# Windowed attention and a gelu MLP on one core: one group of blocks of the first products as seven block products in five more tiles

## The chip, the core and the metric

The kernel runs on 1 core of one Trainium2 chip. The time is the device time of one execution in microseconds (us); lower is better. A core has five engines that run in parallel, each with its own queue of instructions in order: TensorE (PE in the profile; its weight loads are PEld), VectorE (DVE), ScalarE (ACT), GpSimd (POOL) and SyncE (SP), which here only issues DMAs. TensorE writes its results to PSUM, eight banks of 128 x 512 float32; VectorE and ScalarE read them from there. Everything else lies in SBUF. DMAs are issued by SP, by GpSimd and, at the ends, by ScalarE.

## The reference

Attention with a window of 32 positions on each side, over 8 batches of 8 heads, 576 positions and 64 columns per head, then a two-layer MLP with a tanh gelu on the 4608 rows of 512 that come out:

```python
scores = np.matmul(q, k.transpose(0, 1, 3, 2)) / np.sqrt(D)
scores = np.where(np.abs(pos[:, None] - pos[None, :]) <= 32, scores, -1e9)
attn = softmax(scores)
x = (attn @ v).transpose(0, 2, 1, 3).reshape(4608, 512)
h = x @ w_in                                   # 512 -> 2048
g = 0.5 * h * (1 + np.tanh(sqrt(2 / pi) * (h + 0.044715 * h ** 3)))
out = g @ w_out                                # 2048 -> 512
```

## The kernel before

**Tiles and products.** The 4608 rows are cut into nine tiles of 512 (t = 0 to 8). A tile has *first products* (x times w_in, transposed: 16 blocks of 128 columns of w_in, each four matmuls of 512 columns that add up over the 512 inputs in one PSUM bank), then a gelu per block on ScalarE into gT, and *second products* (gT times w_out). While the second products of tile t run, the attention of batch t + 1 is woven in between their matmuls, so that its result xT is there for the next tile. One table per kind of tile (PLAN for tiles 2 to 6) says before which matmul of the second products which step of the attention stands: s a group's scores (TensorE, then the exponential on ScalarE), m the mask (VectorE), v the weighing with the values (TensorE, then ScalarE), x the scaling into xT (VectorE). The instruction order of each engine is written out by hand through these tables.

**Seven instead of eight.** The second products of tiles 1 to 8 are done by a scheme in which a 2 x 2 block product takes seven block products instead of eight, in the form of the table WINO (line 41), with sums and differences of the blocks. sums (line 686) makes S1 to S4 of a part of gT on VectorE, four operations of 128 x 512 per quarter, in pairs called t and u. In tiles 7 and 8 the first products use the same scheme for two groups of four blocks each, A (blocks 4 to 7 by number) and B (8 to 11): in_w (line 591) makes the sums of the weights once, in_x (line 606) the differences T1 to T4 of the tile's xT, in_product (line 616) one block product of four matmuls of 256 columns, and in_mixed (line 632) walks the list MIX, in which "B4" is product 4 of group B, "s" copies a part result from PSUM to the tile sb, "c" adds a part result from PSUM to it, "g" is a gelu, a plain number an ordinary block, "t" and "u" the sums. The sums of weights of group B are made on VectorE in tiles 3 and 4, those of group A in tile 6.

**Begun blocks.** At the end of tile t the first three blocks of tile t + 1 are begun: nine of their matmuls run before the last part of xT is ready, the last three at the start of the first products.

**Keys, queries and values.** For batches from 2 on, queries and keys are loaded as float32 by SP (load_qk, line 180), cast to float16 on VectorE at the start of the tile (turn_queries line 407, turn_keys 416, turn_tails 426 for the last 64 positions) and transposed by DMAs that SP issues. Values of batches from 4 on are loaded as float16 by GpSimd (load_v), those of 2 and 3 as float32 (load_vr, line 402) and cast by GpSimd; pair_v (line 222) copies them to a second place on VectorE. The raw loads share one pool, rawp, with two buffers each for the tags qr and kr.

**GpSimd's queue.** GpSimd issues the stores of the output pieces (line 713), the loads of values (lines 216, 220), and casts. `later` holds the four output pieces of tile 0, in the order 0, 3, 1, 2 of their row blocks; pieces 3 and 2 lie in the pool yp, tag yo, pieces 0 and 1 in hp.

Of the kernel before, what the change touches and what calls it, by code (L numbers as in the profile page):

```python
# [9 lines left out]
FP32 = mybir.dt.float32  # L10
# [26 lines left out]
def cut(b):  # L37
# [7 lines left out]

PLAN = {7: "s0@0 s1@1 v-1", 16: "m0 m1 x-1", 33: "s2@0 v0@1 v1", 36: "m2", 44: "x0", 50: "x1",
        62: "s3@0 s4@1 v2", 66: "m3", 80: "x2", 84: "m4", 91: "v3", 112: "x3"}
# [14 lines left out]
MIX = ("3 g3 A0 s0A B0 s0B 12 g12 A2 B2 cA00 cB00 A1 s1A gA00 A4 B1 s1B gB00 B4 t0 u0 13 g13 A3 s3A B3 s3B 14 g14 "  # L62
       "cA11 cB11 A5 gA10 B5 gB10 gA11 gB11 A6 B6 cA01 cB01 15 gA01 gB01 t1 t2 g15 t3 u1 u2 u3").split()
UNITS = {"A": 1, "B": 2}

# [6 lines left out]


RING = 1536
LOW = -30000.0
# [3 lines left out]
def kernel(  # L79
# [9 lines left out]
    nc = tc.nc  # L89
# [18 lines left out]
    big = ctx.enter_context(tc.tile_pool(name="big", bufs=1))  # L108
    rawp = ctx.enter_context(tc.tile_pool(name="rawp", bufs=2))
    hp = ctx.enter_context(tc.tile_pool(name="hp", bufs=1))  # L110
# [26 lines left out]
    def load_early(b):  # L137


        qr = rawp.tile([128, H, 256], FP32, name="qr")  # L140
        kr = rawp.tile([128, H, 256], FP32, name="kr")
        raws[b] = [qr, kr, None]
# [37 lines left out]
    def load_qk(b):  # L180


        if b == 3:
            qr = raws[3]
        else:
            qr = rawp.tile([128, H, 256], FP32, name="qr")
            load_q(b, qr)
        kr = rawp.tile([128, 4, H, 64], FP32, name="kr")
        if b > 3:
            qt = tailp.tile([16, H, 256], FP32, name="qt", tag="vt")  # L190
            kt = tailp.tile([64, H, 64], FP32, name="kt", tag="tr")
            raws[b] = (qr, kr, qt, kt)
        else:
            raws[b] = [qr, kr, tailp.tile([128, H, 64], FP32, name="tr", tag="tr"), None]
        for c in range(4):
            nc.sync.dma_start(kr[:, c, :, :],
                              k[b, :, 128 * c:128 * c + 128, :].rearrange("h p d -> p h d"))
        load_tails(b, nc.sync)
        if b == 3:
            load_vr(3)  # L200
# [201 lines left out]
    def load_vr(b):  # L402
        vr = vrs[b] = rawp.tile([128, 4, H, 64], FP32, name="qr")
        for c in range(4):
            nc.sync.dma_start(vr[:, c, :, :],
                              v[b, :, 128 * c:128 * c + 128, :].rearrange("h p d -> p h d"))

    def turn_queries(b, src, dst, p0, p1):
        for pr in range(NPAIR):
            nc.vector.tensor_copy(  # L410
                dst[:, pr, :, :, :].rearrange("p j h d -> p h j d"),
                src[:, 2 * pr:2 * pr + 2, :].rearrange("p h (j d) -> p h j d", j=4))
# [3 lines left out]
    def turn_keys(b):  # L416
        k16, kr = halfs[b][1], raws[b][1]
        for pr in range(NPAIR):
            nc.vector.tensor_copy(k16[:, pr, :, :, :], kr[:, :, 2 * pr:2 * pr + 2, :])
            if pr % 2:  # L420
# [4 lines left out]
    def turn_tails(b):  # L425
# [3 lines left out]
        turn_queries(b, qt, qt16, 128, 144)  # L429
        nc.vector.tensor_copy(kt16.rearrange("p r h d -> p (r h d)"), kt.rearrange("p h d -> p (h d)"))  # L430
        nc.sync.dma_start_transpose(
# [159 lines left out]
    def in_w(eng, unit, *which):  # L591
# [3 lines left out]
        if (unit, "s") not in mixed:  # L595
            halves = [(rawp if unit == "A" else yp).tile([128, 2, 2, 2, 128], FP16, name="wc" + unit + str(x),
                                                         tag=("qr", "kr")[x] if unit == "A" else "yo") for x in range(2)]
            mixed[unit, "s"] = [half[:, x] for half in halves for x in range(2)]
        S1, S2, S3, S4 = mixed[unit, "s"]
# [15 lines left out]

    def in_product(unit, n):
        a, w, new = WINO[n]
        if n == 0:
            phs[unit, "a"] = psO.tile([128, 512], FP32, name="pu", tag="O") if unit == "A" else bank(1)
        elif n in (2, 4):  # L620
            which = "b" if n == 2 else "c"
            if unit == "A":
                phs[which] = psS.tile([128, 2, 512], FP32, name="pu2", tag="S1" if n == 2 else "S0")
            phs[unit, which] = phs[which][:, "AB".index(unit), :]
# [7 lines left out]
    def in_mixed(t):  # L632
        if "A" not in mixed:
            mixed["A"] = rawp.tile([128, 3, 512], FP32, name="sa", tag="qr")
            mixed["B"] = rawp.tile([128, 3, 512], FP32, name="sb", tag="kr")

        place = {"00": (0, "b"), "01": (1, "c"), "11": (2, "c")}
        for step in MIX:
            kind, rest = step[0], step[1:]
            if kind in UNITS:  # L640
                in_product(kind, int(rest))
            elif kind == "s":
# [287 lines left out]
    for t in range(NT):  # L930
        b = t + 1
        att = b < B
        if t:
# [8 lines left out]
            elif att:  # L942
                if b > 3:
                    open_and_turn(b)
                turn_keys(b)
                if b > 3:
                    turn_tails(b)
            if t >= NT - 2:
                if t == NT - 2:
                    in_x(t)  # L950
                in_mixed(t)
            for fc in range(begun, NF if t < NT - 2 else 0):
                ffn_in(t, fc)
                if t == 1 and fc == 3:
# [3 lines left out]
                    nc.sync.dma_start(raws[2][4], v[2, :, 512:S, :].rearrange("h p d -> p h d"))  # L958
                    raws[3] = rawp.tile([128, H, 256], FP32, name="qr")
                    load_q(3, raws[3])  # L960
# [9 lines left out]
                if t == 2 and fc == 8:  # L970
                    cast_tails(3, nc.gpsimd.tensor_copy)
                if t == 2 and fc == 13:
                    trans_tails(3, psO.tile([128, 8, 128], FP16, name="pt", tag="O"), copy=nc.scalar.copy,
                                copy_q=nc.scalar.copy)
                if t > 1 and fc == 8 and att:
                    pair_v(b, nc.vector.tensor_copy)
        plan = PLAN_0 if not t else PLAN_1 if t == 1 else PLAN if att else {40: "v-1", 66: "x-1"} if t == B - 1 else {}

# [8 lines left out]
        for i in range(113 if t else 65):  # L987
# [80 lines left out]
            if t == 1 and i in PAIR_1:  # L1068
# [41 lines left out]
```

## Time and profile before

| what | us |
|---|---|
| three runs | 296.19, 297.32, 299.41 (median 297.32) |
| profiled execution | 296.65 |
| its span in the profile | 294.6 |
| TensorE busy, granted clock | 285.9, 0.997 of full |
| VectorE busy | 212.4 |
| ScalarE busy | 196.5 |
| GpSimd busy | 88.8 |

Stages of the tiles in the profiled execution, from TensorE's timeline (the first products from the first begun block on):

| tile | first products | second products |
|---|---|---|
| 2 | 84.76 to 98.91 | 98.91 to 115.10 |
| 3 | 115.10 to 129.32 | 129.32 to 145.93 |
| 4 | 145.93 to 159.74 | 159.74 to 176.41 |
| 5 | 176.41 to 190.22 | 190.22 to 206.82 |
| 6 | 206.82 to 220.64 | 220.64 to 237.24 |

Rows of the profile name the engine, the line of the kernel, the operation and its tiles (out <- in), the shape and type, and how often; then busy us and the mean ns of one, or in a timeline the start and the length in us and, in brackets, how long the engine sat idle before and what released it.

### The profile page before, as it was taken

How to read it: one execution, taken by the hardware profiler on the slowest of the kernel's cores; microseconds unless marked ns; L12 is line 12 of the kernel's file. 1: busy time of each engine (PE TensorE's matmuls, PEld its weight loads, DVE VectorE, ACT ScalarE, POOL GpSimd, SP SyncE). 2: the span in 40 equal slices, each digit the busy share in tenths (PEclk: the TensorE clock that was granted, in tenths of full speed). 3: DMA queues.
4: the chain of work that ended last, by engine and by line, in shares of the span. 5: the costliest groups of instructions: out<-in, count | busy, mean ns of one | idle time of the engine just before them, and what ended most of it. 6: DMA issues, size and time to landing. Idle time of an engine off the chain costs nothing.

```text
span 294.6 us, 7286 instructions
## 1 busy us (share of the span) xinstructions
PE 285.9 (97%) x2945; PEld 192.7 (65%) x2945; DVE 212.4 (72%) x467; ACT 196.5 (67%) x315; POOL 88.8 (30%) x143
## 2 busy tenths in 40 slices
PE   8889999999999999999999999999999999999993
PEld 3535545547765687568755885588558867887783
DVE  4755477998897667858796878686957877865762
ACT  5965877777677874787667776796669558706800
POOL 4445335004228713205250615050800050025000
PEclk9999999999999999999999999999999999999998
DMA  7999998999999998999999999899691040004013
GB/s 229 275 380 396 359 305 196 254 186 203 248 229 202 251 202 188 113 139 245 162 212 94 246 157 191 116 245 154 117 190 7 0 118 28 2 26 120 0 47 99
DMA packets 114392, 51.02 MB, mean 173 GB/s; under 512 B 98471, under 2 KB 110247, under 8 KB 114102
## 3 DMA queue, kind: packets, MB, share of 16 engines
q1 hardware_dynamic: 89460, 38.67, 62.4%
q0 software_dynamic: 23776, 10.83, 23.4%
q10 hardware_dynamic: 1122, 1.06, 1.1%
q8 instruction: 23, 0.38, 0.6%
q14 instruction: 11, 0.09, 0.1%
HBM read 36.70 MB, written 9.44 MB: 157 GB/s over the span
## 4 chain that ended last, share of the span: by engine, by line
PE 85%; DVE 5%; DMA 5%; issue 1%; SPq 1%; ACT 1%; POOL 0%; DVEq 0%
PE mm L751 32%; PE ph L577 17%; PE mm L577 16%; PE ps_s L468 4%; PE pu L629 3%; DMA kr<-in_k_dram 3%; PE mm L723 2%; DMA wst<-in_moe_w_in_dram 2%; PE py L723 2%; PE ps_d L495 2%; PE ps_o L505 2%; DVE t L684 2%; DVE s L694 1%; PE mm L629 1%; PE ps_od L495 1%; PE ps_od L505 1%
## 5 line engine op out<-in xcount | busy, mean ns | idle before, releaser
L577 PEld LDWEIGHTS <-w_in 128*128 128x128 f16 x512 | 57.4, 113 | 49.8 <-POOL w_in L250 1.5
L577 PE MATMUL ph<-xT,w_in 128*128 128x512 f16 x256 | 64.5, 379 | 0.6 <-POOL w_in L250 0.6
L577 PE MATMUL mm<-xT,w_in 128*128 128x512 f16 x256 | 64.1, 379 | 0.0
L585 ACT ACTIVATE gT<-mm 128x512 f16<-128x512 f32 x60 | 35.6, 598 | 33.3 <-PE mm L577 32.7
L713 POOL DMA_DIRECT2D out_dram<-y x55 | 32.8, 605 | 82.4 <-DVE y L780 75.3
L751 PEld LDWEIGHTS <-s 128*128 128x128 f16 x512 | 49.3, 98 | 7.1 <-DVE s L694 0.6
L751 PE MATMUL mm<-t,s 128*128 128x256 f16 x376 | 45.2, 273 | 0.2 <-DVE y L764 0.2
L694 DVE TENSOR_TENSOR s<-gT 128x512 f16<-128x512 f16 x64 | 27.5, 430 | 19.1 <-ACT gT L585 18.9
L751 PEld LDWEIGHTS <-gT 128*128 128x128 f16 x384 | 36.2, 98 | 6.4
L585 ACT ACTIVATE gT<-ph 128x512 f16<-128x512 f32 x58 | 32.4, 604 | 10.9 <-PE ph L577 10.9
L481 ACT ACTIVATE pe<-ps_s 128x960 f16<-128x960 f32 (+1 forms) x31 | 29.5, 975 | 13.2 <-PE ps_s L468 13.1
L751 PE MATMUL mm<-w_out,gT 128*128 128x256 f16 x256 | 32.6, 273 | 0.0
L104 ACT ACT_TABLE_LOAD x18 | 23.1, 1283 | 2.2 <-issue 1.9
L530 ACT ACTIVATE lt<-ps_d 128x480 f32<-128x480 f32 (+2 forms) x28 | 15.6, 556 | 10.4 <-PE ps_d L495 6.9
L531 ACT ACTIVATE lt<-lt 128x480 f32<-128x480 f32 (+3 forms) x36 | 21.1, 585 | 1.1
L490 DVE TENSOR_TENSOR pe<-pe,band 128x960 f16<-128x960 f16 x28 | 18.5, 680 | 2.0 <-ACT pe L481 1.9
L505 PEld LDWEIGHTS <-V 128*64 128x64 f16 x520 | 13.7, 111 | 5.5 <-DVE V L226 1.5
L751 PE MATMUL mm<-t,gT 128*128 128x256 f16 x128 | 16.1, 273 | 0.0
L694 DVE TENSOR_TENSOR s<-s,gT 128x512 f16<-128x512 f16 x32 | 14.0, 436 | 1.1
L216 POOL DMA_DIRECT2D V<-in_v_dram x16 | 14.3, 908 | 1.1 <-PE ps_s L468 0.4
L751 PE MATMUL mm<-w_out,s 128*128 128x256 f16 x120 | 14.6, 273 | 0.0
L540 DVE TENSOR_TENSOR xT<-ps_o,lt 128x480 f16<-128x480 f32 (+5 forms) x26 | 13.4, 535 | 1.6 <-PE ps_o L505 1.6
(149 smaller groups left out, 390.3 us busy)
## 6 DMA issues: line engine op xcount, KB each, us to landing
kr<-in_k_dram SPq DMA_DIRECT2D x31, 256.0 KB, 10.2
qr<-in_q_dram SPq DMA_DIRECT2D x6, 1024.0 KB, 5.9
wst<-in_moe_w_in_dram SPq DMA_DIRECT2D x8, 512.0 KB, 6.6
wst<-in_moe_w_out_dram SPq DMA_DIRECT2D x2, 1024.0 KB, 10.5
wst<-in_moe_w_out_dram SPq DMA_DIRECT2D x4, 512.0 KB, 7.4
qr<-in_v_dram SPq DMA_DIRECT2D x8, 256.0 KB, 6.5
V<-in_v_dram POOLq DMA_DIRECT2D x16, 128.0 KB, 8.5
qr<-in_q_dram SPq DMA_DIRECT2D x7, 256.0 KB, 7.3
```

The source lines that it names most:

```text
L104: nc.scalar.add_instruction(mybir.InstLoadActFuncSet(name=nc.get_next_instruction_name(), act_func_set_id=which, ins=[], outs=[]))
L216: nc.gpsimd.dma_start(V[:, c, :, :], v[b, :, 128 * c:128 * c + 128, :].rearrange("h p d -> p h d"))
L481: nc.scalar.activation(pe, ps[:, :, 0:w], AF.Exp, scale=SCALE)
L490: nc.vector.tensor_tensor(pe, pe, m.rearrange("k (o j) p -> k o j p", o=1).broadcast_to(list(pe.shape)), op=ALU.mult)
L505: nc.tensor.matmul(o[64 * h:64 * h + 64, cols].rearrange("d (j p) -> d j p", j=4)[:, :, p0 - q0:p1 - q0], Vs[b % 2][:, slot, 2 * pr + h, : ...
L530: nc.scalar.activation(lt[:, 0:n], d[:, 0:n], AF.Ln)
L531: nc.scalar.activation(lt[:, 0:n], lt[:, 0:n], AF.Exp, scale=-1.0)
L577: nc.tensor.matmul(ph, w_cols[:, dc, fc // 4, fc % 4, :], xT[:, dc, t * 512 % RING:t * 512 % RING + 512], start=(dc == 0), stop=(dc == 3))
L585: nc.scalar.activation(gTs[t][:, fc, :], phs[fc], AF.Gelu_apprx_tanh)
L694: nc.vector.tensor_tensor(dst, x, y, op=op)
L713: eng.dma_start(out_v[b, j, q0 + p:q0 + p + e, cols], yo[m:m + e, cols])
L751: nc.tensor.matmul(pys["apart"][:, 0:256] if apart else py[:, blk, :], lhsT, wino[w][:, f, :], start=(new and i % (8 if one else 16) == 0) ...
```

## The change

Group B of the first products is done as seven block products in tiles 2 to 6 too (LONE = 2 and the list MIX_1; the other twelve blocks stay as they are). In these tiles the first part result lies in the bank O instead of x1, since `alone` is set. Because the sums of group B's weights are needed from tile 2 on, they are made in tile 1's second products, by GpSimd. The casts of the keys and of the tails of batches 4 to 7 go from VectorE to GpSimd. The pool rawp has one buffer each for four tags (q0, q1, k0, k1), so that sb has a place of its own from tile 2 on (in q1) and the differences of x lie in k0 or k1 in tiles 2 to 6. Tile 0's output pieces of the pool yp are stored in tile 1, the other two in tile 2. The weighing of group 1 stands at matmul 36 instead of 33. In the ordinary blocks' place stand the list's steps "pair" (pair_v) and "tails" (tile 2's transposes of batch 3's tails).

```diff
-PLAN = {7: "s0@0 s1@1 v-1", 16: "m0 m1 x-1", 33: "s2@0 v0@1 v1", 36: "m2", 44: "x0", 50: "x1",
+PLAN = {7: "s0@0 s1@1 v-1", 16: "m0 m1 x-1", 33: "s2@0 v0@1", 36: "m2 v1", 44: "x0", 50: "x1",
...
+MIX_1 = ("3 B0 g3 s0B 4 B2 cB00 B1 s1B g4 5 g5 6 g6 t0 u0 B3 s3B gB00 pair B4 7 g7 cB11 gB11 12 g12 t1 u1 B5 gB10 B6 cB01 gB01 13 g13 14 g14 t2 u2 tails 15 g15 t3 u3").split()
+LONE = 2
...
-    rawp = ctx.enter_context(tc.tile_pool(name="rawp", bufs=2))
+    rawp = ctx.enter_context(tc.tile_pool(name="rawp", bufs=1))
...
-            qr = rawp.tile([128, H, 256], FP32, name="qr")
+            qr = rawp.tile([128, H, 256], FP32, name="qr", tag="q0")
             load_q(b, qr)
-        kr = rawp.tile([128, 4, H, 64], FP32, name="kr")
+        kr = rawp.tile([128, 4, H, 64], FP32, name="kr", tag="k1" if b == 3 else "k0")
...
-        vr = vrs[b] = rawp.tile([128, 4, H, 64], FP32, name="qr")
+        vr = vrs[b] = rawp.tile([128, 4, H, 64], FP32, name="vr", tag="q1")
...
     def turn_queries(b, src, dst, p0, p1):
         for pr in range(NPAIR):
-            nc.vector.tensor_copy(
+            (nc.gpsimd if p0 and b > 3 else nc.vector).tensor_copy(
...
-            nc.vector.tensor_copy(k16[:, pr, :, :, :], kr[:, :, 2 * pr:2 * pr + 2, :])
+            (nc.gpsimd if b > 3 else nc.vector).tensor_copy(k16[:, pr, :, :, :], kr[:, :, 2 * pr:2 * pr + 2, :])
...
-        nc.vector.tensor_copy(kt16.rearrange("p r h d -> p (r h d)"), kt.rearrange("p h d -> p (h d)"))
+        (nc.gpsimd if b > 3 else nc.vector).tensor_copy(kt16.rearrange("p r h d -> p (r h d)"), kt.rearrange("p h d -> p (h d)"))
...
-        xc = hp.tile([128, 4, 2, 256], FP16, name="xc", tag="q16" if t % 2 else "k16")
+        xc = rawp.tile([128, 4, 2, 256], FP16, name="xc", tag="k1" if t > 2 else "k0") if t < NT - 2 else \
+            hp.tile([128, 4, 2, 256], FP16, name="xc", tag="q16" if t % 2 else "k16")
...
-            phs[unit, "a"] = psO.tile([128, 512], FP32, name="pu", tag="O") if unit == "A" else bank(1)
+            phs[unit, "a"] = psO.tile([128, 512], FP32, name="pu", tag="O") if unit == "A" or alone else bank(1)
...
-        if "A" not in mixed:
-            mixed["A"] = rawp.tile([128, 3, 512], FP32, name="sa", tag="qr")
-            mixed["B"] = rawp.tile([128, 3, 512], FP32, name="sb", tag="kr")
+        if "B" not in mixed:
+            mixed["B"] = rawp.tile([128, 3, 512], FP32, name="sb", tag="q1")
+        if t == NT - 2:
+            mixed["A"] = rawp.tile([128, 3, 512], FP32, name="sa", tag="k0")
...
-        for step in MIX:
+        for step in MIX if t >= NT - 2 else MIX_1:
...
+                if t >= LONE:
+                    in_x(t)
                 turn_keys(b)
+                if b == 3:
+                    cast_tails(3, nc.gpsimd.tensor_copy)
...
+            elif t >= LONE:
+                in_mixed(t)
-            for fc in range(begun, NF if t < NT - 2 else 0):
+            for fc in range(begun, NF if t < LONE else 0):
...
-            if t in (3, 4) and i == 52:
-                in_w(nc.vector, "B", *((1, 2) if t == 3 else (3, 4)))
+            if t == LONE - 1 and i == 40:
+                in_w(nc.gpsimd, "B", 1, 2, 3, 4)
...
-            if t == 2 and i in (40, 44):
-                store(0, *later[1 if i == 40 else 3])
+            if t == 2 and i in (8, 12):
+                store(0, *later[0 if i == 8 else 2])
             if t == 1 and i == 30:
                 cast_vt(2)
-                store(0, *later[0])
-                store(0, *later[2])
+                store(0, *later[1])
+                store(0, *later[3])
```

More of the change, by code (lines that the diff above doesn't have):

```diff
@@ L137, in load_early @@
     def load_early(b):
-        qr = rawp.tile([128, H, 256], FP32, name="qr")
-        kr = rawp.tile([128, H, 256], FP32, name="kr")
+        qr = rawp.tile([128, H, 256], FP32, name="qr", tag=f"q{b}")
+        kr = rawp.tile([128, H, 256], FP32, name="kr", tag=f"k{b}")
         raws[b] = [qr, kr, None]
@@ L185, in load_qk @@
         else:
-            qr = rawp.tile([128, H, 256], FP32, name="qr")
+            qr = rawp.tile([128, H, 256], FP32, name="qr", tag="q0")
             load_q(b, qr)
-        kr = rawp.tile([128, 4, H, 64], FP32, name="kr")
+        kr = rawp.tile([128, 4, H, 64], FP32, name="kr", tag="k1" if b == 3 else "k0")
         if b > 3:
@@ L595, in in_w @@
         if (unit, "s") not in mixed:
-            halves = [(rawp if unit == "A" else yp).tile([128, 2, 2, 2, 128], FP16, name="wc" + unit + str(x),
-                                                         tag=("qr", "kr")[x] if unit == "A" else "yo") for x in range(2)]
-            mixed[unit, "s"] = [half[:, x] for half in halves for x in range(2)]
+            if unit == "A":
+                wc = rawp.tile([128, 4, 2, 2, 128], FP16, name="wcA", tag="q0")
+                mixed[unit, "s"] = [wc[:, x] for x in range(4)]
+            else:
+                halves = [yp.tile([128, 2, 2, 2, 128], FP16, name="wcB" + str(x), tag="yo") for x in range(2)]
+                mixed[unit, "s"] = [half[:, x] for half in halves for x in range(2)]
         S1, S2, S3, S4 = mixed[unit, "s"]
@@ L614, in in_x, with in_product @@
             nc.vector.tensor_tensor(dst, a, b, op=ALU.subtract)
-    def in_product(unit, n):
+    def in_product(unit, n, alone):
         a, w, new = WINO[n]
         if n == 0:
-            phs[unit, "a"] = psO.tile([128, 512], FP32, name="pu", tag="O") if unit == "A" else bank(1)
+            phs[unit, "a"] = psO.tile([128, 512], FP32, name="pu", tag="O") if unit == "A" or alone else bank(1)
         elif n in (2, 4):
             which = "b" if n == 2 else "c"
-            if unit == "A":
+            if unit == "A" or alone:
                 phs[which] = psS.tile([128, 2, 512], FP32, name="pu2", tag="S1" if n == 2 else "S0")
@@ L632, in in_mixed @@
     def in_mixed(t):
-        if "A" not in mixed:
-            mixed["A"] = rawp.tile([128, 3, 512], FP32, name="sa", tag="qr")
-            mixed["B"] = rawp.tile([128, 3, 512], FP32, name="sb", tag="kr")
+        if "B" not in mixed:
+            mixed["B"] = rawp.tile([128, 3, 512], FP32, name="sb", tag="q1")
+        if t == NT - 2:
+            mixed["A"] = rawp.tile([128, 3, 512], FP32, name="sa", tag="k0")
         place = {"00": (0, "b"), "01": (1, "c"), "11": (2, "c")}
-        for step in MIX:
+        for step in MIX if t >= NT - 2 else MIX_1:
             kind, rest = step[0], step[1:]
-            if kind in UNITS:
-                in_product(kind, int(rest))
+            if step == "pair":
+                pair_v(t + 1, nc.vector.tensor_copy)
+            elif step == "tails":
+                if t == 2:
+                    trans_tails(3, psO.tile([128, 8, 128], FP16, name="pt", tag="O"), copy=nc.scalar.copy,
+                                copy_q=nc.scalar.copy)
+            elif kind in UNITS:
+                in_product(kind, int(rest), t < NT - 2)
             elif kind == "s":
@@ L958 @@
                     nc.sync.dma_start(raws[2][4], v[2, :, 512:S, :].rearrange("h p d -> p h d"))
-                    raws[3] = rawp.tile([128, H, 256], FP32, name="qr")
+                    raws[3] = rawp.tile([128, H, 256], FP32, name="qr", tag="q0")
                     load_q(3, raws[3])
@@ L969 @@
                                 copy_q=nc.scalar.copy)
[L970 to L976, printed above, removed]
         plan = PLAN_0 if not t else PLAN_1 if t == 1 else PLAN if att else {40: "v-1", 66: "x-1"} if t == B - 1 else {}
```

## The prediction

> **What bounds the kernel now.** I read the page first: busy times, then the chain that ended last.
>
> ```profile
> PE 285.9 (97%) x2945; PEld 192.7 (65%) x2945; DVE 212.4 (72%) x467; ACT 196.5 (67%) x315; POOL 88.8 (30%) x143
> ...
> PE 85%; DVE 5%; DMA 5%; issue 1%; SPq 1%; ACT 1%; POOL 0%; DVEq 0%
> ```
>
> TensorE is busy 97% of the span and holds 85% of the chain. Then the busy times by stage, here the first products of tiles 2 and 4 (columns: window, length, then busy us of PE, PEld, DVE, ACT, POOL with instruction counts, granted clock, DMA share, GB/s):
>
> ```profile
> 84.76:98.91 14.15, 14.15 (x70) 7.36 (x69) 10.34 (x23) 10.18 (x18) 9.36 (x15) 1.00 1.13 204
> 145.93:159.74 13.81, 13.81 (x66) 7.23 (x65) 11.13 (x29) 8.70 (x16) 5.76 (x10) 1.00 1.08 153
> ```
>
> TensorE has no idle time there, at full clock. So a column taken off TensorE shortens the span, and any wait put in front of TensorE lengthens it by its whole length: nothing later makes it good. The other engines have 2.7 us (VectorE) and more to spare per stage, but in order, so where that time lies counts.
>
> **What is saved.** The timeline of TensorE prices both kinds of matmul (start, length, instruction), the 512-column blocks in tile 4 and the block products that tile 7 already runs:
>
> ```profile
> 149.38 1.89 PE L577 MATMUL mm<-xT,w_in 128*128 128x512 f16 x8
> 151.11 1.03 PE L577 MATMUL ph<-xT,w_in 128*128 128x512 f16 x4
> ...
> 242.57 1.04 PE L629 MATMUL pu<-xT,w_in 128*128 128x256 f16 x8
> 243.44 1.04 PE L629 MATMUL pu<-xc,wcA 128*128 128x256 f16 x8
> ```
>
> From start to start eight blocks' matmuls take 1.73 us, 0.216 each; eight of the products take 0.87 us, 0.109 each. Per tile 16 x 0.216 = 3.46 us go and 28 x 0.109 = 3.05 us come: 0.41 us saved, in five tiles 2.05 us. This is the whole possible gain; TensorE waits for nothing else in these tiles.
>
> **What is added to ScalarE and VectorE.** ScalarE gets two copies per tile of 0.58 us (the copies to sb). It is busy 8.7 of 13.8 us and now waits 0.27 us before nearly each gelu; the copies fit there, so I cost them at nothing (uncovered they would be 1.2 us a tile). VectorE:
>
> ```profile
> L614 DVE TENSOR_TENSOR xc<-xT 128x512 f16<-128x512 f16 x4 | 1.7, 416 | 0.0
> L644 DVE COPY sb<-mm 128x512 f32<-128x512 f32 x2 | 1.4, 680 | 0.0
> L649 DVE TENSOR_TENSOR sb<-pu,sb 128x512 f32<-128x512 f32 x6 | 4.1, 680 | 0.0
> ```
>
> Four differences of 0.42 us, a copy of 0.68 and three additions of 0.68 make 4.4 us; the key and tail casts of tiles 3 to 6 (1.4 + 1.5 + 0.4 us, L419, L410, L430) leave it. The load hardly changes; the order does. Take tile 4, where the three begun blocks' last matmuls start at 147.87 (t). Product 0 ends at t + 0.65 + 0.86 + 0.44, product 1 is due at t + 3.25 = 151.12. VectorE ends the previous tile's additions at 146.9, casts the queries to 148.3, makes the differences to 149.8 and the first copy to sb by 150.7: no wait. Product 6 is due at t + 8.45 = 156.3 and needs the addition of product 4. VectorE reaches that after the addition of product 2 (151.9), four sums of S (1.5), the two copies of V (0.69 + 0.55) and itself (0.69): 155.5. **So 0.85 us is spare before product 6**, if VectorE runs at its usual pace. The removed sums of weights in tiles 3 and 4 (0.68 us each) lay beside idle time: nothing.
>
> **What GpSimd does to VectorE.** Now nine casts per tile (3 to 6) run on GpSimd, behind its stores of the previous tile (in tile 4 from 145.37 to 151.69), so just beside those sums and copies. Tile 2 of the trace shows such a meeting, first GpSimd, then VectorE:
>
> ```profile
> 87.17 1.74 POOL L993 CAST V<-qr 128x512 f16<-128x512 f32 x2 [5.87 <-DMA qr<-in_v_dram]
> 89.83 1.50 POOL L993 CAST V<-qr 128x512 f16<-128x512 f32 x2 [0.92 <-DMA qr<-in_v_dram]
> ```
> ```profile
> 89.68 0.42 DVE L694 TENSOR_TENSOR s<-s,gT 128x512 f16<-128x512 f16 x1
> 90.03 0.83 DVE L694 TENSOR_TENSOR s<-gT 128x512 f16<-128x512 f16 x1
> 90.78 0.82 DVE L694 TENSOR_TENSOR s<-gT,s 128x512 f16<-128x512 f16 x1
> ```
>
> Beside the casts the sums start 0.75 us apart; alone they start 0.34 apart (152.29, 152.63). Each f16 operation of VectorE in SBUF that meets a cast loses 0.41 us. (Operations that read PSUM show no loss: L540 takes 0.66 us at 51.52 beside two casts.) Six such operations lie before product 6's addition: 6 x 0.41 = 2.46, less 0.85 spare: TensorE waits 1.6 us. Where the stores end earlier (tiles 3 and 5) one of the six escapes: 5 x 0.41 - 0.85 = 1.2. I take 1.4 a tile, 5.6 us in four. From below: with two meetings or fewer it is nothing. From above: the late gelus behind it also hold the bank of block 13, which the second products start in, 0.2 to 0.75 us more.
>
> The Trainium skill (SBUF — State Buffer, Who interferes with whom) says that a VectorE instruction with two SBUF inputs and a GpSimd instruction reading SBUF exclude each other for the whole instruction. By it six meetings would cost six whole casts, 6 x 0.61 - 0.85 = 2.8 us a tile; the trace agrees that they exclude each other, and shows 0.41 for one.
>
> **Tile 2.** The first copy writes sb, which now takes the memory of batch 3's values, so in the changed program it waits for GpSimd's casts of them (L993). Those end at 91.33 at the earliest, since the last values land just before 90.6. The copy then ends at 92.0; product 1 is due at 84.76 + 9 x 0.216 + 3.25 = 89.96. TensorE waits 2.1 us at least. The four sums of weights on GpSimd come before those casts. They write over tile 0's output pieces, whose stores are issued at 79.27 and 80.01 and take 4.9 us or more to land, so they start near 84.2. No row shows GpSimd adding two tensors: between a cast's 0.61 us and twice that for twice the inputs, they end at 86.6 to 89.1; with the tail load (0.75) and four casts (0.61 to 0.75) the values are cast by 91.3 to 92.8, and the key casts on VectorE meet them, up to two more times 0.41 and the copy. That is 2.1 to 4.4 us of wait; I take 3.0, nearer the lower end because the sums may start in time. Queued behind the waiting copy on VectorE are the addition of product 2, the first sums of S and the copies of V; behind GpSimd's sums stand, after the casts, tile 1's stores (5 us) and batch 3's tail casts, which TensorE's tail transposes want. In the trace that cast ended at 96.89 and the transposes began at 96.95; now it ends at 96.9 to 98.4, and TensorE, 3 us late, gets there near 100: covered by the wait before it, and up to 1.1 us if that wait is gone.
>
> The Trainium skill (GPSIMD Engine Reference, 3.1) gives some 2.6 cycles per element at 1.2 GHz for two inputs, an estimate of 1.1 us for 512; the wait would then be about 4 us, and no run here shows it yet.
>
> **SP's queue.** The key transposes now wait for GpSimd. In tile 4:
>
> ```profile
> 148.41 3.56 SPq L413 DMA_TRANSPOSE QT<-q  x1
> 152.07 6.22 SPq L421 DMA_TRANSPOSE KT<-k  x2
> ```
>
> The first could be issued after two casts, 151.69 + 1.3 = 153.0, 0.9 us later; landing takes up to 7.6 us (tile 2), so 160.6, and the scores want it at 160.60, now 0.41 earlier. Behind 1.4 us of wait this costs nothing; without it, up to 0.4. The next loads sit behind the second transpose, which holds the queue to 158.3 anyway; keys have one buffer now, but GpSimd's nine casts end near 158 and the load into it is issued at 161.5. The swap of tile 0's stores and the weighing of group 1 three matmuls later move work into stretches where both queues sat idle: nothing.
>
> **Sum.** -2.05 + 3.0 + 5.6 = +6.55 us. The profiled execution took 296.65 us (span 294.6, 2.05 around it), 0.67 under the median of 297.32: 303.2 us.
>
> **Rivals.** *Only tile 2 waits* (0.20): the casts fall into VectorE's 2.7 us of idle, fewer than three meetings before product 6. For it: GpSimd's stores meet fewer VectorE casts and may end sooner. Against: VectorE has no idle between the additions of products 2 and 4. -2.05 + 3.0 = 297.6 (296.7 to 299.0).
> *All is covered* (0.17), not slower: as above, and batch 3's casts end before 89.2 so that the copy is ready by 89.96. That takes loads landing some 2 us sooner than they did: 296.65 - 2.05 = 294.6.
> *The transposes become the wait* (0.08): the slack of 0.9 at the scores is gone, 0.4 to 1.0 us in four tiles besides tile 2: 299.2 to 301.6.
> *My forecast*, both waits: 0.55; from 4 x 1.2 + 2.1 (301.5) to 4 x 2.3 + 4.4 (308.2).
>
> **Chances.** One per cent, 3 us, is about what a measurement tells from no change. Slower: 0.55 and part of the third rival, 0.58. Faster needs more than the whole saving: 0.05. Same: 0.37. The range 294 to 307 takes in the covered case and leaves out the top of the forecast.
>
> **What would show it.** Block products at 0.109 us and 16 fewer block matmuls a tile; TensorE idle before product 1 in tile 2 with VectorE as releaser, behind GpSimd; in tiles 3 to 6 idle before product 6, and L694 and L225 above 0.7 us beside GpSimd's casts. I am wrong if those operations keep 0.42 us or TensorE keeps its 13.8 - 0.41 us per stage.

## The result, and the profile after

| | us |
|---|---|
| kernel before, 6 runs | median 297.37 (296.15 to 299.41) |
| changed kernel, 6 runs | median 309.64 (307.43 to 310.37) |
| ratio, 95% interval | 1.0403 (1.0353 to 1.0453) |
| profiled execution of the changed kernel | 309.71, span 307.7 |

The change costs 12.3 us, where the prediction said 5.9 over the median of before, and the time lies above its range, which ended at 307. Slower was the forecast; by how much was not. Ratios, here and below, leave out runs in the machine's slower state (one of 314.25 us in the fourth experiment, one of the kernel before beside the last two) and go by the kernel before on the same chip, with medians of 298.36 us beside the first four experiments, 297.43 beside the next four and 297.97 beside the last two. The page first:

```profile
PE 288.9 (94%) x3005; PEld 198.6 (65%) x3005; DVE 231.6 (75%) x467; ACT 198.0 (64%) x325; POOL 119.1 (39%) x183
...
PE 71%; DVE 15%; DMA 7%; issue 3%; SPq 1%; ACT 1%; POOL 0%; DVEq 0%
```

TensorE's share of the chain falls from 85 to 71%, VectorE's rises from 5 to 15%: TensorE now waits for VectorE. Where, the lengths of the stages tell (from the starts on TensorE's timeline; "other" is the time up to tile 2 and after tile 6):

| stage | before | after | difference |
|---|---|---|---|
| tile 2, first products | 14.15 | 20.39 | +6.24 |
| tile 3, first products | 13.81 | 14.76 | +0.95 |
| tile 4, first products | 13.81 | 15.02 | +1.21 |
| tile 5, first products | 13.81 | 14.76 | +0.95 |
| tile 6, first products | 13.81 | 16.00 | +2.19 |
| second products of tiles 2 to 6, each (tile 4) | 16.60 (16.67) | 16.82 (16.88) | +0.22, five times |
| other | | | +0.5 |

The last row is not put down to the change: the part up to tile 0's second products, in which the weights are loaded, takes 32.7 to 34.6 us in the twelve profiled executions, with no order by kernel. The table of stages ahead of the prediction has tile 3 begin at 115.10; on the timeline its first begun block starts at 115.51, which makes its stages 13.81 and 16.60 like the others.

TensorE's waits in the changed kernel, from its timeline (start, length, instruction, then in brackets how long it sat idle before and what released it):

```profile
89.71 0.38 PE L579 MATMUL mm<-xT,w_in 128*128 128x512 f16 x1 [2.24 <-DVE xT L542]
95.62 0.76 PE L635 MATMUL pu<-xc,wcB 128*128 128x256 f16 x4 [2.50 <-DVE sb L657]
134.13 0.60 PE L635 MATMUL pu<-xT,wcB 128*128 128x256 f16 x4 [1.00 <-DVE sb L662]
165.68 0.60 PE L635 MATMUL pu<-xT,wcB 128*128 128x256 f16 x4 [0.96 <-DVE sb L662]
197.61 0.60 PE L635 MATMUL pu<-xT,wcB 128*128 128x256 f16 x4 [0.99 <-DVE sb L662]
230.43 0.60 PE L635 MATMUL pu<-xT,wcB 128*128 128x256 f16 x4 [2.23 <-DVE sb L662]
```

The brackets count from a matmul's modelled end; from start to start, less the usual spacing, the losses are 2.40 and 2.66 us in tile 2 and 1.17, 1.13, 1.16 and 2.40 in tiles 3 to 6. The last four stand before product 6 and are released by the addition of product 4 to sb, as predicted. The second stands before product 1, where the prediction had a wait too, but for another cause, as will be seen. The first was not foreseen.

**Tile 2.** VectorE there, in the kernel before (start, length of the group, instruction):

```profile
83.28 1.42 DVE L410 CAST q<-qr 128x512 f16<-128x512 f32 x4
```

and in the changed one:

```profile
83.88 5.31 DVE L412 CAST q<-qr 128x512 f16<-128x512 f32 x4
89.11 0.71 DVE L542 TENSOR_TENSOR xT<-ps_o,lt 128x384 f16<-128x384 f32 x2
...
91.22 1.28 DVE L620 TENSOR_TENSOR xc<-xT 128x512 f16<-128x512 f16 x1
...
93.54 1.43 DVE L421 CAST k<-kr 128x512 f16<-128x512 f32 x4
94.89 0.67 DVE L657 COPY sb<-pu 128x512 f32<-128x512 f32 x1
```

And GpSimd:

```profile
83.15 1.51 POOL L609 TENSOR_TENSOR wcB<-w_in 128x512 f16<-128x512 f16 x1 [2.05 <-DMA out_dram<-yo]
84.74 1.24 POOL L609 TENSOR_TENSOR wcB<-wcB,w_in 128x512 f16<-128x512 f16 x1
85.93 1.69 POOL L609 TENSOR_TENSOR wcB<-w_in 128x512 f16<-128x512 f16 x1
87.58 1.33 POOL L609 TENSOR_TENSOR wcB<-w_in,wcB 128x512 f16<-128x512 f16 x1
...
89.57 2.64 POOL L1005 CAST V<-vr 128x512 f16<-128x512 f32 x4
```

Four casts of batch 3's queries, 1.42 us before, take 5.31: one cast for each of GpSimd's four sums, each cast over only as the sum beside it ends. Behind the casts in VectorE's queue stands the scaling of xT (L542) that TensorE needs for the begun blocks. And everything after it on VectorE is 3.9 us late. The first of the differences of x (L620) loses another 0.86 us beside the casts of the values (1.28 instead of 0.42). So the copy to sb begins at 94.89, behind VectorE's own casts of the keys, while the casts of the values, which the prediction took for its releaser, had ended at 92.2.

Then the clock. The windows view of the changed kernel, twice in tile 2 and once in tile 6 (window, length, busy us of PE, PEld, DVE, ACT, POOL, granted clock, DMA share, GB/s):

```profile
87.00:90.00 3.00, 0.76 (x5) 0.30 (x3) 3.00 (x5) 0.00 (x0) 3.00 (x4) 1.00 0.97 165
...
95.62:99.46 3.84, 3.84 (x13) 1.65 (x12) 3.73 (x7) 1.68 (x3) 2.33 (x4) 0.56 0.98 190
230.40:234.00 3.60, 3.54 (x20) 2.06 (x20) 2.84 (x8) 3.13 (x7) 0.00 (x0) 1.00 0.91 143
```

After the second wait TensorE runs at 0.56 of its clock for 3.84 us: 512-column matmuls start 0.427 us apart instead of 0.216, and 1.7 us are lost with no wait in sight. So tile 2 loses 2.40 + 2.66 + 1.7 us and saves 0.39, 6.4 in all, of which the stages show 6.24. After tile 6's wait, nearly as long, the clock stayed full; the last section has the reason. Of the six runs the shortest, 307.43 us, had a mean clock of 1.000, the others 0.993 or 0.994.

**Tile 4.** VectorE between the additions of products 2 and 4 (the last line is the addition that TensorE waits for), and GpSimd:

```profile
160.16 0.72 DVE L707 TENSOR_TENSOR s<-gT 128x512 f16<-128x512 f16 x1
160.91 0.72 DVE L707 TENSOR_TENSOR s<-s,gT 128x512 f16<-128x512 f16 x1
161.55 0.82 DVE L707 TENSOR_TENSOR s<-gT 128x512 f16<-128x512 f16 x1
162.30 0.82 DVE L707 TENSOR_TENSOR s<-gT,s 128x512 f16<-128x512 f16 x1
163.14 1.01 DVE L227 COPY V<-V 64x2048 f16<-64x2048 f16 x1
164.16 0.87 DVE L228 COPY V<-V 64x1536 f16<-64x1536 f16 x1
164.95 0.67 DVE L662 TENSOR_TENSOR sb<-pu,sb 128x512 f32<-128x512 f32 x1
```

```profile
159.40 2.69 POOL L421 CAST k<-kr 128x512 f16<-128x512 f32 x4
162.04 3.60 POOL L412 CAST qt<-qt 16x512 f16<-16x512 f32 x4
```

The six operations that the prediction named are longer by 0.30, 0.30, 0.40, 0.40, 0.32 and 0.32 us, 2.04 together (predicted 2.46). Less the 0.85 us that were spare, that makes 1.19 of wait; measured 1.13. In tiles 3 and 5 all six are longer too (2.08 us together in tile 3, from 128.57 on), though the prediction let one of them escape. In tile 6 the first of them starts beside the first of GpSimd's four casts of the keys and outlasts all four (223.08 to 225.36):

```profile
223.65 1.99 DVE L707 TENSOR_TENSOR s<-gT 128x512 f16<-128x512 f16 x1
```

### The profile page after: what moved, and what is told of

Its sections match the earlier page's. It is cut to its first block, busy times and chain, and to the rows that moved or that the text cites. A ratio compares the mean times of both kernels' runs of the same rounds, so it can differ in the third digit from the quotient of the medians.

```text
span 307.7 us, 7481 instructions
## 1 busy us (share of the span) xinstructions
PE 288.9 (94%) x3005; PEld 198.6 (65%) x3005; DVE 231.6 (75%) x467; ACT 198.0 (64%) x325; POOL 119.1 (39%) x183
## 4 chain that ended last, share of the span: by engine, by line
PE 71%; DVE 15%; DMA 7%; issue 3%; SPq 1%; ACT 1%; POOL 0%; DVEq 0%
PE mm L764 31%; PE ph L579 11%; PE mm L579 8%; PE pu L635 5%; DVE s L707 5%; PE ps_s L470 3%; DMA kr<-in_k_dram 3%; DMA wst<-in_moe_w_in_dram 2%; PE mm L736 2%; PE ps_d L497 2%; PE py L736 2%; DVE q L412 2%; DVE sb L662 2%; PE ps_o L507 2%; DVE t L697 1%
## 5 line engine op out<-in xcount | busy, mean ns | idle before, releaser
L579 PEld LDWEIGHTS <-w_in 128*128 128x128 f16 x432 | 48.6, 114 | 41.6 <-issue 4.2
L726 POOL DMA_DIRECT2D out_dram<-y x55 | 31.0, 573 | 86.3 <-DVE y L793 75.0
L579 PE MATMUL ph<-xT,w_in 128*128 128x512 f16 x236 | 60.2, 383 | 0.9 <-POOL w_in L252 0.9
L579 PE MATMUL mm<-xT,w_in 128*128 128x512 f16 x196 | 51.8, 384 | 2.2 <-DVE xT L542 2.2
L707 DVE TENSOR_TENSOR s<-gT 128x512 f16<-128x512 f16 x64 | 31.5, 492 | 6.1 <-ACT gT L666 3.5
L587 ACT ACTIVATE gT<-mm 128x512 f16<-128x512 f32 x20 | 11.7, 600 | 26.2 <-PE mm L579 26.1
L587 ACT ACTIVATE gT<-ph 128x512 f16<-128x512 f32 x33 | 18.0, 606 | 5.9 <-PE ph L579 5.9
L666 ACT ACTIVATE gT<-sb 128x512 f16<-128x512 f32 x21 | 13.4, 636 | 10.6 <-DVE sb L662 10.6
L670 ACT ACTIVATE gT<-ph 128x512 f16<-128x512 f32 x26 | 15.6, 601 | 4.3 <-PE ph L579 4.3
L635 PEld LDWEIGHTS <-wcB 128*128 128x128 f16 x112 | 11.0, 98 | 10.9 <-issue 8.8
L670 ACT ACTIVATE gT<-mm 128x512 f16<-128x512 f32 x29 | 16.2, 593 | 1.4 <-PE mm L579 0.6
L662 DVE TENSOR_TENSOR sb<-pu,sb 128x512 f32<-128x512 f32 x21 | 14.3, 682 | 3.7 <-PE pu L635 2.4
```

Of the source, the lines that this page charges most:

```text
L579: nc.tensor.matmul(ph, w_cols[:, dc, fc // 4, fc % 4, :], xT[:, dc, t * 512 % RING:t * 512 % RING + 512], start=(dc == 0), stop=(dc == 3))
L587: nc.scalar.activation(gTs[t][:, fc, :], phs[fc], AF.Gelu_apprx_tanh)
L635: nc.tensor.matmul(ps[:, 256 * h:256 * h + 256], lhs[:, d, h, :], rhs[:, d, :], start=(n in (0, 2, 4) and h == d == 0), stop=(h == d == 1) ...
L662: nc.vector.tensor_tensor(x, phs[rest[0], which], x, op=ALU.add)
L670: nc.scalar.activation(gTs[t][:, fc, :], phs[fc], AF.Gelu_apprx_tanh)
L707: nc.vector.tensor_tensor(dst, x, y, op=op)
```

## The experiments

All but one start from the changed kernel; "GpSimd's casts alone" starts from the kernel before. In the diffs, - is the kernel that the experiment starts from; the two mends at the end are shown against the order of "Tiles 3 to 6 alone". The cuts in the diffs are marked by dots.

**The sums of weights earlier.**

```diff
                 if t == 1 and fc == 3:
+                    store(0, *later[1])
+                    store(0, *later[3])
...
             if t == 1 and i == 30:
                 cast_vt(2)
-                store(0, *later[1])
-                store(0, *later[3])
+                in_w(nc.gpsimd, "B", 1, 2, 3, 4)
...
-            if t == LONE - 1 and i == 40:
-                in_w(nc.gpsimd, "B", 1, 2, 3, 4)
```

> Tile 0's two pieces are stored in tile 1's first products and the sums of weights are made by GpSimd some 9 us earlier, at matmul 30 of tile 1's second products; nothing else changes. Theory (in the changed kernel GpSimd's sums hold VectorE's casts of batch 3's queries, 5.31 us instead of 1.42, and all of tile 2's loss hangs on that): the casts take 1.4 to 1.8 us, the wait of 2.4 us before the last matmuls of tile 2's begun blocks is gone, TensorE's clock stays full, product 1 still waits 1.0 to 2.3 us: 303 to 306 us. Rival (the prediction's step: the values of batch 3 come late and hold the copy to sb): product 1 starts no earlier than the casts of the values allow, so most of the wait moves to product 1, 4 us and more there: 307.5 us or above.

308.14 us, ratio 1.0314 (1.0260 to 1.0368). Tile 2 is cured: its first products take 13.97 us, the queries' casts 1.46, there is no wait before the begun blocks and 0.2 us before product 1, the clock stays full. But the second products of tile 1 now take 20.89 us instead of 16.91. VectorE beside the sums, now at 75.1 to 80.7 (copies of batch 2's values, 0.42 us each in the changed kernel):

```profile
74.68 2.21 DVE L227 COPY V<-V 64x1024 f16<-64x1024 f16 x1
76.90 1.29 DVE L228 COPY V<-V 64x768 f16<-64x768 f16 x1
...
78.81 0.90 DVE L227 COPY V<-V 64x1024 f16<-64x1024 f16 x1
79.72 1.28 DVE L228 COPY V<-V 64x768 f16<-64x768 f16 x1
```

TensorE waited 2.36 us for the second of them, and after that its clock stood at 0.58 for 3.8 us, 1.6 us lost; in tile 6 seven matmuls at half clock came on top, 1.5 us. So the queries' casts and tile 2's waits hang on the sums, which is the theory; the expected time was missed because the sums hold whatever VectorE does beside them, and there TensorE waited too. The rival, the values' casts as the cause, is out as far as this goes; as tile 2 begins 3.6 us later here, it does not show what they would cost if nothing else were late.

**The casts left out.** The nine casts of GpSimd are left out for batches 5 to 7, whose keys and tails are then batch 4's.

```diff
-                    hp.tile([128, NPAIR, 4, 2, 64], FP16, name="k16")]
+                    hp.tile([128, NPAIR, 4, 2, 64], FP16, name="k16") if b < 5 else halfs[4][1]]
...
-        for pr in range(NPAIR):
+        for pr in range(0 if p0 and b > 4 else NPAIR):
```

(and the same for the key casts and the tails, which keep batch 4's tiles.)

> The nine casts of keys and tails on GpSimd are left out for batches 5 to 7, that is in tiles 4 to 6 (the transposes read batch 4's); tile 3 keeps them. Theory (the casts slow VectorE's float16 operations before product 6's addition): tile 3 keeps its wait of 1.2 us before product 6, tiles 4, 5 and 6 lose theirs (1.13, 1.16 and 2.40) and the 0.2 to 0.5 us before the second products, sum 5.6: 304 us. Rival (VectorE's order is too full by itself, the 0.85 us to spare was miscounted): over 0.8 us of wait stays in each of the tiles 4 to 6, and the time is 307 us or above.

304.97 us, ratio 1.0217 (1.0166 to 1.0268). Tiles 3 and 4 in the windows view, the first with its casts, the second without:

```profile
124.80:139.57 14.77, 13.74 (x78) 8.30 (x77) 13.14 (x26) 8.69 (x18) 10.69 (x18) 1.00 0.89 154
156.40:169.81 13.41, 13.41 (x78) 8.29 (x76) 10.95 (x26) 8.71 (x18) 5.25 (x10) 1.00 0.87 163
```

The same 26 instructions of VectorE take 13.14 us beside the casts and 10.95 without, and TensorE's 1.36 us of loss is gone, in tiles 5 and 6 too (13.42 each). The casts are the cause; the order alone costs nothing.

**Another order.**

```diff
-MIX_1 = "... g6 t0 u0 B3 s3B gB00 pair B4 7 g7 cB11 gB11 12 g12 t1 u1 B5 gB10 B6 cB01 gB01 13 g13 ... 15 g15 t3 u3"
+MIX_1 = "... g6 B3 s3B gB00 B4 7 g7 cB11 gB11 t0 u0 12 g12 B5 gB10 B6 cB01 gB01 t1 u1 13 g13 ... 15 g15 t3 u3 pair"
```

> The list of the tiles 2 to 6 is reordered: the first sums of S (t0 u0) stand behind the addition of product 4, the second sums behind that of product 6, and the copies of the values at the list's end. Theory (product 6 waits only because those sums and copies stand before the addition in VectorE's queue): the waits before product 6 in tiles 3 to 6 go (5.9 us in all), at most 0.5 us a tile comes back before the second products that read the last sums: 303 to 305.5 us. Rival (beside the casts VectorE has too much to do in the stage, wherever it stands): the wait only moves to the second products, 308 us or above.

303.98 us, ratio 1.0186 (1.0138 to 1.0234). Tiles 3 and 4, and tile 4's second products:

```profile
121.32:134.74 13.42, 13.42 (x79) 8.28 (x78) 9.76 (x23) 9.02 (x18) 9.28 (x17) 1.00 1.08 140
151.62:165.04 13.42, 13.42 (x79) 8.30 (x78) 9.65 (x23) 8.77 (x18) 10.47 (x19) 1.00 0.93 155
165.04:183.01 17.97, 17.08 (x267) 13.80 (x266) 14.67 (x31) 13.10 (x19) 5.14 (x7) 1.00 1.24 180
```

VectorE in tile 4, with the addition that product 6 waits for, and the sums now behind it:

```profile
160.28 0.69 DVE L662 TENSOR_TENSOR sb<-pu,sb 128x512 f32<-128x512 f32 x1 [2.58 <-ACT sb L657]
160.89 0.74 DVE L707 TENSOR_TENSOR s<-gT 128x512 f16<-128x512 f16 x1
161.66 0.71 DVE L707 TENSOR_TENSOR s<-s,gT 128x512 f16<-128x512 f16 x1
```

The waits before product 6 are gone with the casts still there: VectorE is idle before the addition and does it in time. Most of the casts now run while VectorE is idle, and only two of the four sums are longer; so the order takes away meetings as well as what was queued behind them, and this run does not part the two. In tile 4 1.1 us and in tile 6 0.5 us come back in the second products, where the copies of the values, now last, are still running: a part of the rival, in two tiles of four.

**The weighing back at 33.**

```diff
-PLAN = {... 33: "s2@0 v0@1", 36: "m2 v1", ...
+PLAN = {... 33: "s2@0 v0@1 v1", 36: "m2", ...
```

> The weighing of group 1 stands at matmul 36 no more, but at 33 beside that of group 0, as in the kernel before. Theory (a changeover from the second products to a weighing and back costs 0.22 us, which the second products of tiles 2 to 6 show in full): 5 x 0.22 = 1.1 us less, 308.5 us. Rival (the later place hides a wait for the mask of group 1 behind VectorE's work, and the 0.22 comes from elsewhere): the wait is back at matmul 33, no less than now, 309.6 us or above.

310.98 us (308.99 to 314.25), ratio 1.0395 (1.0334 to 1.0455): by its time the theory missed, but the time cannot tell 1.1 us here, as TensorE waited once for 6.0 us in tile 2 of the profiled execution and ran 5.95 us at half clock after it. There the stores of tile 0's pieces landed later, GpSimd's sums ran from 85.83 to 91.6, and what they held was not the queries' casts (1.42 us) but the four differences of x, 5.6 us in sum instead of 1.7; VectorE's casts of the keys then took 3.08 us beside the casts of the values, and the copy to sb, at 95.38, waited its last 0.50 us for those, which is the wait of the prediction. So the sums hold whatever VectorE does beside them, here in the same place of the program. The stage can tell the 1.1 us. Tile 3's second products in the changed kernel:

```profile
137.34:154.16 16.82, 16.82 (x267) 13.75 (x266) 12.26 (x23) 13.17 (x19) 5.32 (x7) 1.00 1.25 177
```

and here:

```profile
138.91:155.51 16.60, 16.60 (x267) 13.85 (x267) 12.23 (x23) 13.17 (x19) 5.26 (x7) 1.00 1.28 182
```

The same 267 matmuls without idle time, about 0.22 us less in each of the five tiles (in tile 2 0.15). TensorE pays that for going over from the second products to a weighing and back once more: in the changed kernel the 14 matmuls at the end of group 0's weighing take 0.33 us to the next start instead of 0.23, and the three second products before group 1's take 0.44 instead of 0.33.

**GpSimd's casts alone, in the kernel before.**

```diff
-            nc.vector.tensor_copy(k16[:, pr, :, :, :], kr[:, :, 2 * pr:2 * pr + 2, :])
+            (nc.gpsimd if b > 3 else nc.vector).tensor_copy(k16[:, pr, :, :, :], kr[:, :, 2 * pr:2 * pr + 2, :])
```

(and the same for the tails.)

> The kernel before with one part of the change: the casts of keys and tails of batches 4 to 7 on GpSimd. Theory (the casts slow VectorE's float16 operations by 0.3 to 0.4 us each, and that costs only where an addition that TensorE waits for stands behind them): L694 and L225 grow in the tiles 3 to 6, TensorE waits for nothing, the time is within 1 us of the kernel before. Rival (VectorE's sums come too late for the second products, or the transposes of the keys too late for the scores): 0.5 to 2 us a tile, 2 to 8 us slower.

297.64 us, ratio 0.9994 (0.9961 to 1.0028). The sums of S from tile 3 to 6 here:

```profile
L694 DVE TENSOR_TENSOR s<-gT 128x512 f16<-128x512 f16 x32 | 20.2, 632 | 12.0 <-ACT gT L585 12.0
L694 DVE TENSOR_TENSOR s<-s,gT 128x512 f16<-128x512 f16 x16 | 10.0, 628 | 0.6
```

and in the kernel before:

```profile
L694 DVE TENSOR_TENSOR s<-gT 128x512 f16<-128x512 f16 x32 | 13.4, 419 | 13.0 <-ACT gT L585 13.0
L694 DVE TENSOR_TENSOR s<-s,gT 128x512 f16<-128x512 f16 x16 | 6.8, 425 | 0.6
```

10.0 us more on VectorE in these two groups alone, and no difference in the time. But VectorE is rid of its own casts in return (5.9 + 5.9 + 1.6 us in the kernel before), so that its busy time hardly moves, 213.5 us beside 212.4. In this order the casts cost nothing. Whether that is because no addition that TensorE waits for stands behind the lengthened sums, or because VectorE has less to do than in the changed kernel, this run does not tell; the third experiment shows that with the changed kernel's work, too, the order is enough.

**The sums of weights on VectorE**, at the place of the first experiment (nc.vector in place of nc.gpsimd).

> As e1 (sums of weights at matmul 30 of tile 1's second products), but the four sums on VectorE. Theory (GpSimd's sums hold VectorE for the whole of each): VectorE alone makes them in 1.7 to 2.7 us, so tile 1's second products take 16.9 + 0 to 2.0 us instead of the 20.89 that they take with GpSimd; 2 to 4 us under e1. Rival (the sums' work costs the same wherever it is done): 20 us and more there, as e1.

309.04 us, ratio 1.0407 (1.0372 to 1.0443). Tile 1's second products take 19.94 us: the four sums occupy VectorE from 74.76 to 78.07 and TensorE waits 2.87 us for what stands behind them. This goes against the theory's number: at that place the sums cost about as much on either engine. The clock stayed full; without the 1.6 us of reduced clock the first experiment's 20.89 would have been the shorter. Tile 1's first products also took 1.4 us longer here, behind a late load of keys. And though no sums run beside tile 2, TensorE waited 0.89 us before product 1 there: the queries' casts took 2.07 us beside two of the values' casts.

**Tiles 3 to 6 alone, in a better order.** LONE = 3; VectorE makes the sums of weights in tile 2's second products; the copies of the values keep their old place, only the first sums of S move.

```diff
-LONE = 2
+LONE = 3
...
-MIX_1 = "... g6 t0 u0 B3 s3B gB00 pair B4 7 g7 cB11 gB11 12 g12 t1 u1 B5 gB10 B6 cB01 gB01 13 g13 ..."
+MIX_1 = "... g6 B3 s3B gB00 pair B4 7 g7 cB11 gB11 t0 u0 12 g12 B5 gB10 B6 cB01 gB01 t1 u1 13 g13 ..."
...
-            if t == LONE - 1 and i == 40:
-                in_w(nc.gpsimd, "B", 1, 2, 3, 4)
+            if t == 2 and i in (52, 86):
+                in_w(nc.vector, "B", *((1, 2) if i == 52 else (3, 4)))
```

(with v1 back at matmul 33, and tile 2's ordinary blocks and their steps as before.)

> Block products in tiles 3 to 6 alone; the sums of weights are made by VectorE in tile 2's second products (two at matmul 52, two at 86); the first sums of S stand behind the addition of product 4, the copies of the values stay before it; group 1's weighing is back at matmul 33. Theory (these three places are all that the change lost): tile 2 takes what it took before (14.15 and 16.60 us), the first products of tiles 3 to 6 take 13.42 instead of 13.81, their second products 16.60: 1.56 us less than the kernel before, ratio 0.995 (0.992 to 0.999). Rival (the casts on GpSimd keep VectorE busy into the second products): 0.5 to 1.1 us more in tiles 4 and 6, ratio 0.999 to 1.004.

297.63 us, ratio 1.0005 (0.9982 to 1.0029). Tiles 3 and 5 take 13.42 us, tile 2 and all second products what they took before, but tiles 4 and 6 take 13.74 and 13.99. Neither theory had the reason. ScalarE in tile 4:

```profile
159.98 0.63 ACT L666 ACTIVATE gT<-sb 128x512 f16<-128x512 f32 x1 [1.20 <-DVE sb L662]
160.52 1.06 ACT L670 ACTIVATE gT<-mm 128x512 f16<-128x512 f32 x2
```

It waits 1.20 us for the addition of product 6, which stands behind the lengthened sums; the next gelu, block 13's, frees the bank in which the second products start, and TensorE waits 0.3 to 0.6 us for it.

**The same with tile 2** and GpSimd's sums, as the change has them (LONE = 2, otherwise the order above).

> The changed kernel with the same order of the list and the same place of the weighing, but with tile 2 and GpSimd's sums of weights as the change has them. Theory: what is left over e5 is tile 2's loss alone, its waits before the begun blocks and before product 1 and the half clock behind them: 4 to 8.5 us over e5, 300 to 305 us. Rival (tile 2's loss came from the same sums and copies in VectorE's queue as in the tiles 3 to 6): it goes with the new order, within 2 us of e5.

301.99 us, ratio 1.0149 (1.0121 to 1.0177), 4.4 us over the one before: tile 2's first products take 20.54 us instead of 14.15, again with two waits (2.79 and 2.24 in brackets) and 3.8 us at 0.58 of the clock. (That is 6.4 more; but the profiled execution of the one before took 1.9 us longer up to tile 1, so that the two spans lie 4.6 apart.)

**Two mends of that order.** One moves the second pair of the first sums of S behind the addition of product 6:

```diff
-"... cB11 gB11 t0 u0 12 g12 B5 gB10 B6 cB01 gB01 t1 u1 13 g13 14 ..."
+"... cB11 gB11 t0 12 g12 B5 gB10 B6 cB01 gB01 u0 t1 u1 13 g13 14 ..."
```

> As e5, but of the first sums of S the second pair (u0) stands behind the addition of product 6. Theory (what e5 lacks are the waits of 0.3 us in tile 4 and 0.6 in tile 6 before the second products: VectorE's addition of product 6 comes late behind the sums, ScalarE waits 1.2 us for it and the gelu of block 13 holds the bank): both waits go, the first products take 13.42 us in all of the tiles 3 to 6, 1.56 us under the kernel before, ratio 0.995 (0.992 to 0.998). Rival (the sums pushed back are late for the second products): 0.3 to 0.8 us a tile comes back there, ratio 0.998 to 1.004.

296.13 us beside 297.97 of the kernel before on the same chip: ratio 0.9942 (0.9911 to 0.9973), **0.6% below the kernel before**. That is little, but the interval leaves out 1. The four first products:

```profile
118.32:131.73 13.41, 13.41 (x78) 8.30 (x76) 10.82 (x24) 9.01 (x18) 10.90 (x17) 1.00 0.98 173
148.70:162.11 13.41, 13.41 (x78) 8.31 (x76) 10.77 (x23) 9.01 (x18) 11.45 (x19) 1.00 0.95 158
178.78:192.20 13.42, 13.42 (x79) 8.31 (x78) 11.20 (x23) 8.95 (x18) 10.22 (x17) 1.00 1.02 165
208.80:222.22 13.42, 13.42 (x79) 8.31 (x78) 11.91 (x23) 9.01 (x18) 11.60 (x18) 1.00 0.92 166
```

0.39 us saved in each, with GpSimd's casts beside them all. Tile 3's second products are 0.36 longer in this execution, those of the other three unchanged.

The other lets ScalarE do block 13's gelu first ("cB01 t1 u1 13 g13 gB01 14" in place of "cB01 gB01 t1 u1 13 g13 14").

> As e5, but ScalarE does the gelu of block 13 before the one that waits for the addition of product 6; VectorE's order is that of e5. Theory (the same as for e9: the gelu of block 13 is late only because it is queued behind one that waits): 13.42 us in the first products of the tiles 3 to 6, ratio 0.995 (0.992 to 0.998). Rival (ScalarE has no room, the next bank is late instead): the waits before the second products of tiles 4 and 6 stay at 0.3 us or more, ratio as e5.

296.99 us, ratio 0.9979 (0.9948 to 1.0010): 13.42 in all four too, but tile 6's second products take 17.29 instead of 16.60: 0.7 of the 1.56 us came back there, a stage later than the rival had it. The interval takes in 1.

## Why the prediction was wrong

**The saving** was sized rightly: 0.41 a tile foretold, 0.39 measured wherever nothing waits (13.81 to 13.42).

**Tiles 3 to 6** went as predicted, in place, cause and nearly in size: six operations lengthened before the addition of product 4, 0.85 us to spare, a wait before product 6. Predicted 1.4 a tile, with 0.2 to 0.75 more for the late gelu of block 13 kept as the upper end; measured with both 1.34, 1.60, 1.34 and 2.58, together 6.9 against 5.6. Tile 6 has the excess: its first sum met the casts' start and took 1.99 us. That tiles 3 and 5 came out at the predicted 1.2 us of wait is partly luck: six operations lost 0.35 us each there, where the prediction had five losing 0.41. Leaving the casts out and reordering the list each remove these waits, so the cause is shown from two sides.

**Tile 2 is the step that failed.** The prediction had 3.0 us, a wait of the copy to sb for the casts of the values; 6.6 were lost. That the wait before product 1 is 2.66 us, close to the 3.0, is luck: the casts of the values ended at 92.2, as foretold, and the copy began 2.7 us after that, when VectorE came to it. The sums of weights were costed only by when they end ("86.6 to 89.1"; they ended at 88.9) and by the delay that they hand on along GpSimd's queue. What they do to VectorE beside them was not asked: GpSimd's casts had been given a price of 0.41 us per operation that they meet, the sums none, though VectorE's casts of the queries lie in just that stretch and carry the scaling of xT behind them. They cost 3.9 us there, which became two waits of TensorE, and 1.7 us of half clock behind the second, for which the prediction had no term.

The Trainium skill (SBUF — State Buffer, Who interferes with whom) had said that an instruction of VectorE that needs the ports shared with GpSimd and one of GpSimd exclude each other for a whole instruction. For the sums that is what the trace shows, 5.31 us for four casts beside four sums; for GpSimd's casts it mostly shows less, 0.30 to 0.40 a meeting, while one such cast takes 0.60 to 0.64 alone. But it also shows more, 0.86 us beside two casts in tile 2 and 1.57 beside four in tile 6. The 2.8 us of wait a tile that the prediction worked out from the rule were not reached: 1.13 to 1.17 in three tiles, 2.40 in the fourth.

**The moved weighing** was put at nothing because both queues are idle there. TensorE itself pays 0.22 us for the extra changeover, 1.1 in all, and the prediction had not priced that.

**The rivals.** The key transposes never became the wait: with the casts on GpSimd and no other wait, the first and the second products take 13.42 and 16.60 us. That only tile 2 would wait, or nothing, fell with tiles 3 to 6. Sum of the terms as measured: -1.95 + 6.6 + 6.9 + 1.1 = 12.6 us, and with the 0.5 that lie elsewhere the 13.1 by which the span grew.

What stays open: what the values' casts in q1 would cost tile 2 if VectorE were on time, of which there are only the traces of 0.50 and 0.89 us named above; and whether a place exists before tile 2 where the sums cost nothing, other than the two that were tried.

## What to carry to other kernels

Before work goes to an idle engine, list what the other engine does beside it, operation by operation, and what stands behind the last of those in its queue: here the same nine casts a tile cost TensorE 6.9 us in four tiles in one order, and next to nothing in another, in which fewer of VectorE's operations met them and none held up an addition. Where the bound engine waits for a short addition, put that addition ahead of work that is only needed a stage later; the same casts and products cost nothing in tiles 3 to 6, and the kernel comes out 0.6% below the one before, once the list has the additions first, tile 2 is left alone and the sums of weights lie where VectorE has time. And a step that is moved between matmuls also costs the matmul engine its changeover.

## What the runs showed of the hardware

TensorE's granted clock fell to half after some of its waits (from start to start 2.48, 2.51, 2.57, 2.77, 3.07, 3.71 and 6.25 us), and not after others of the same length (2.31, 2.48, 2.50, 2.62, 3.14, 3.17). Where a trace has two such stretches, whole steps of 3.413 us lie between their starts: 77.97 and 228.16 us in the first experiment, 44.0 steps; 95.24 and 231.77 in the fourth, 40.0. The half clock at the very end, when TensorE has run dry, starts on the same steps, and where a trace has no other it alone fixes them. Within the run each stretch lasts one step, save once two. Cut each trace into these steps, and what counts is how long TensorE is idle, by the modelled ends, within one step:

| trace | step, us | idle in it, us | clock in the next step |
|---|---|---|---|
| changed kernel, first wait of tile 2 | 85.67 to 89.08 | 1.6 | full |
| changed kernel, second wait of tile 2 | 92.49 to 95.91 | 2.5 | half |
| changed kernel, wait of tile 6, its two steps | 225.62 to 229.03, 229.03 to 232.44 | 0.8, 1.4 | full |
| sums of weights earlier, tile 1 | 74.56 to 77.97 | 2.1 | half |
| sums of weights on VectorE, tile 1, its two steps | 73.54 to 76.95, 76.95 to 80.36 | 1.1, 1.8 | full |
| tiles 2 to 6 in the better order | 91.57 to 94.98 | 2.0 | half |

From tile 1 on, before the end, half clock set in after all eight steps with 2.0 us idle or more, and after none with 1.8 or less; once, in the fourth experiment, it stayed for a second step, the first having been idle for 0.9 us. So a wait that falls across two steps can leave the clock full, while one of the same length that lies within a step cost 1.5 to 1.7 us more than its length, and 3.0 where half clock lasted two steps. In the first 25 us the bound is less clear: half clock set in after a step with 1.55 us idle, with two waits of 1.45 and 1.05 us, in one trace and not after one with 1.85 in another. The Trainium skill (TensorE: Matmul & The Clock Gate, What's actually happening) puts this at an idle window of about 3.4 us that runs freely; the traces agree on the length and on its running freely, but 2.0 us of idle time in it were enough.

GpSimd's addition of two float16 tensors of 128 x 512 took 1.24 to 1.69 us with VectorE's casts beside it, more than the 1.1 of the prediction's estimate, against 0.68 to 0.69 on VectorE for the same sums in the kernel before. GpSimd's cast of that size took 0.60 to 0.64 us where no VectorE operation between tensors in SBUF was held beside it, and up to 0.97 in tile 2 where one was.
